# Filler matmuls in and behind the first expert's routing of an attention and mixture-of-experts kernel

## The chip, the cores and the metric

The kernel runs on one core of a Trainium2 chip. The metric is the device time of one execution in microseconds (us). TensorE (PE) does the matrix products, VectorE (DVE) and ScalarE (ACT) the elementwise work, GpSimd (POOL) the indirect transfers, SyncE (SP) issues most of the others. TensorE's clock has two levels, 2.4 GHz (a granted clock of 1.00 in the profile) and 1.2 GHz (0.50).

## The reference

Causal window attention over 8 batches, 8 heads, 576 positions of width 64, followed by a mixture of 8 experts over the 4608 tokens that come out. The experts are filled greedily, best logit first, 576 tokens each:

```python
logits = x @ w_gate                      # x: 4608 x 512, the attention's output
for idx in np.argsort(-logits.flatten()):
    tok, e = idx // E, idx % E
    if assigned[tok] >= 0 or counts[e] >= cap:
        continue
    assigned[tok] = e; counts[e] += 1
for e in range(E):
    mask = assigned == e
    out[mask] = np.maximum(x[mask] @ w1[e], 0.0) @ w2[e]
```

All is in float32. The products of the experts are split in a high and a low part, with three matmuls in place of one.

## The kernel before, in words

The attention runs first, in 36 steps. Then the routing finds which tokens go to which expert, one expert after the other. For expert number p (`Routing.steps`) it searches a threshold in eight rounds (the loop over `r`). In a round of the first expert DVE compares all best logits with 15 candidate thresholds in four pieces (`compare`, line 469), PE counts the hits with 36 matmuls of 8 columns (line 538, into the PSUM tile `rps`), DVE turns the counts into 15x8 flags (`pr`, line 623), one matmul of 8 columns adds them up over the partitions (line 626, tile `h`), and DVE derives the next thresholds from it (lines 641 and 649). Nothing of the next round can begin before that.

After the eight rounds DVE marks the chosen tokens, two matmuls of 72 columns rank them (lines 702 and 703), DVE and ACT spread the ranks into the tiles `A`, `R` and `B`, 18 matmuls of 64 columns make the list (line 744, two halves of nine, each behind its half of `R` and `B`), and eight small ones (line 753) bring it into the form `idx`, by which POOL gathers the expert's 576 rows of x in five transfers (line 1012). PE transposes each gathered tile (line 936), ACT and DVE split it, and the first expert's products follow. From then on the routing of the next experts is recorded between the products of the present one.

While the first expert is routed there is no other work for PE: the attention has ended, and the products wait for the rows. Line 476 (`warm`) fills some of this time. It issues n matmuls of 288 columns whose result nobody reads: 28 behind the list's last matmuls, and 6 behind the transposes of the first gathered tile.

PE runs its instructions in the order in which they are recorded. The order across the concurrent pieces comes from a small planner (`Streams`): each piece is a generator that yields how long it thinks its last work takes. `warm` yields nothing and adds no time to the planner's account. PSUM tiles come from pools with a fixed number of buffers: one `rps` for the routing, three `h` and two `o` for the experts.

Of the kernel before, what the change touches and what calls it, by code (L numbers as in the profile page):

```python
# [9 lines left out]
FT = mybir.dt.float32  # L10
# [15 lines left out]
DM = H * D  # L26
# [265 lines left out]
def consts(tc, cp):  # L292
    nc = tc.nc
    c = dict(pool=cp, zero=cp.tile([128, 128], BF, name="zero"))

    c["jp"] = cp.tile([128, 128], I32, name="jp")
    c["rel"] = cp.tile([128, 128], I32, name="rel")
    nc.gpsimd.iota(c["jp"], pattern=[[1, 128]], base=0, channel_multiplier=-1)
    return c
# [61 lines left out]
class Routing:  # L361
# [107 lines left out]
        self.nc.vector.tensor_tensor(G[:, j0:j1], self.m[:, j0:j1, None].to_broadcast(n),  # L469
                                     thr.bitcast(FT)[:, None, :].to_broadcast(n), OP.is_ge)  # L470

    def warm(self, n):

        x = self.room(128, 288)
        for _ in range(n):
            self.nc.tensor.matmul(x, self.ones, self.r18[:, 0:8], start=True, stop=True)

    def room(self, n, w, spare=False):

        x = self.spare() if spare else self.ps.tile([128, 512], FT, name="rps")  # L480
        return x[0:n, 0:w]
# [12 lines left out]
    def steps(self, p):  # L494
# [8 lines left out]
        if p < E - 1:  # L503
# [19 lines left out]
            for r in range(NR):  # L523
# [71 lines left out]
                if own:  # L595
                    mx = tile_([128, 2], FT, name="mx")
                    nc.vector.tensor_reduce(mx[:, 0:1], cnt, axis=AX.X, op=OP.max)
                    nc.vector.tensor_scalar(mx[:, 1:2], mx[:, 0:1], 0.0, step, op0=OP.is_ge, op1=OP.mult)
                    yield self.dve(350)
                    nc.vector.transpose(pt, mx[:, 1:2].to_broadcast([128, 32]))  # L600
                    d = tile_([128, 1], I32 if r else FT, name="d" if r else "d0")
                    with nc.allow_low_precision(reason="one of 15 multiples of a power of two"):
                        nc.vector.tensor_reduce(d, pt[:, 0:ND], axis=AX.X, op=OP.add)
                    yield self.dve(400) + slack
                    thr2 = tile_([128, ND + 1], I32, name="thr")
                    if r:
                        nc.vector.scalar_tensor_tensor(thr2, self.tab0[:, r + 1], d[:, 0:1],
                                                       base[:, 0:1].to_broadcast([128, ND + 1]),
                                                       op0=OP.bitwise_xor, op1=OP.bitwise_xor)
                    else:  # L610
                        oh = tile_([128, ND], FT, name="oh0")
                        nc.vector.scalar_tensor_tensor(oh, self.dgf, d, thr.bitcast(FT), op0=OP.is_equal, op1=OP.mult,
                                                       accum_out=base.bitcast(FT))
                        nc.vector.tensor_tensor(thr2, self.tab0[:, 1], base[:, 0:1].to_broadcast([128, ND + 1]),
                                                OP.bitwise_xor)
                    base = thr2[:, 0:1]
                    thr = thr2 if r == NR - 2 else thr2[:, 1:]
                    rest = []
                    yield self.dve(300 if r else 500)
                    continue  # L620
                else:
                    pr = tile_([ND, E], BF, name="pr")
                    nc.vector.tensor_scalar(pr, cnt[0:ND], 0.0 if p else float(CAP), step, op0=OP.is_ge, op1=OP.mult)
                    yield self.dve(220) + slack
                    num = self.room(128, E, not p)
                    nc.tensor.matmul(num, self.ones[0:ND], pr, start=True, stop=True)
                    yield self.busy(110) + 200 + slack
                thr2 = tile_([128, ND + 1], I32, name="thr")[:, 0:ND]
                if r == 0:
# [71 lines left out]
        pos = self.room(128, 2 * NJ, not p)  # L701
        nc.tensor.matmul(pos, self.tri, Xf, start=True, stop=False)
        nc.tensor.matmul(pos, self.ones, run, start=False, stop=True)
        yield self.busy(150) + 200 + slack
        Y = tile_([128, 2, NJ], FT, name="Y", bufs=1)
        nc.vector.scalar_tensor_tensor(Y.rearrange("p k j -> p (k j)"), pos, 1.0, Xf,
# [30 lines left out]
        for j0, j1 in ((0, NJ),) if p else ((0, 18), (18, 36)):  # L737
            n = j1 - j0
# [13 lines left out]
            for h in range(2):  # L752
                nc.tensor.matmul(ip[32 * g:32 * g + 32], ils[:, :, h], self.s5[:, h, g], start=(h == 0), stop=(h == 1))
        if p == 0:
            self.warm(28)
        yield self.busy(100) + 200 + slack
        idx = self.rt.tile([128, 5], U32, name=f"idx{p}")
        nc.vector.tensor_copy(idx, ip)
# [58 lines left out]
class Experts:  # L817
# [20 lines left out]

    def room(self):
        return self.ps.tile([128, 320], FT, name="h", bufs=3)  # L840

    def prime(self):

        x = self.fw.tile([8, DM], FT, name="ot", bufs=3)
        self.nc.gpsimd.indirect_dma_start(out=x, out_offset=None, in_=self.xs,
                                          in_offset=IndirectOffsetOnAxis(ap=self.rows[0:8, 0:1], axis=0))
# [460 lines left out]
def body(tc, q, k, v, vt, wg, w1, w2, xs, out):  # L1307
    nc = tc.nc
    with ExitStack() as ctx:
        cp = ctx.enter_context(tc.tile_pool(name="cp", bufs=1))  # L1310
        ctx.enter_context(tc.manual_schedule())
        c = dict(identr=cp.tile([128, 128], FR, name="identr"))
        L = cp.tile([128, NJ, E], FT, name="L")
        rt = Routing(ctx, tc, c, L)
        with ExitStack() as actx:
            ap = actx.enter_context(tc.tile_pool(name="ap", bufs=1))
            c.update(consts(tc, ap))
            wgs = ap.tile([128, HP, 32], FT, name="wgs")
            attention(actx, tc, c, q, k, v, vt, (wgs, wg), xs, L, lambda j0, j1: rt.choices(j0, j1, 0), rt.setup,
                      rt.counters)  # L1320
        rt.start()
        ex = Experts(ctx, tc, c, xs, w1, w2, out)
        rt.spare = ex.room

        st = Streams()
        ex.spawn, ex.busy, rt.busy = st.add, st.busy, st.busy
        ex.clock = rt.clock = lambda: st.now
        ex.warm, ex.rows, rt.prime = rt.warm, rt.rows, ex.prime

        def route():  # L1330
            for p in range(E):
                for dt in rt.steps(p):
                    if p in rt.eint and p not in known:
                        known.add(p)
                        st.add(ex.load(p, rt.eint[p]))
                    if p in rt.idx and p not in listed:
                        listed.add(p)
                        st.add(ex.turn(p, rt.idx[p]))
                    yield dt

        def products():
            for p in range(E):
                yield lambda: p in ex.XT
                yield from ex.steps(p, rt.idx[p])

        known, listed = set(), set()
        st.add(route())
        st.add(products())
        st.run()
# [17 lines left out]
```

## Time and profile before

| what | value |
|---|---|
| median of three runs | 645.01 us (643.61 to 645.83) |
| profiled execution | 644.78 us |
| its span, first to last instruction | 643.1 us |
| mean granted TensorE clock | 0.977 |
| PE busy | 607.8 us, 95% of the span |
| DVE, ACT, POOL busy | 461.0, 340.6, 218.8 us |

The profiled execution takes 1.7 us more than its span. The busy time of PE is an average over three parts: the attention (to about 145 us), the first expert's routing (to about 176 us), and the products of the experts.

### The profile page before, as it was taken

Reading aid. Unit: us, or ns where it says so; the run is one execution under the profiler, and the core shown is the slowest. Engines: PE = TensorE matmul, PEld = TensorE weight load, DVE = VectorE, ACT = ScalarE, POOL = GpSimd, SP = SyncE. Lnnn points to the kernel's source line nnn. Section 1 sums busy time; section 2 is a strip of 40 time slices with the busy share of each in tenths; the row PEclk is TensorE's granted clock in tenths of the full one; section 3 lists DMA queues with packets and bytes.
Section 4 is the critical chain, followed back from the end, with each engine's and each line's share of the span. In section 5 each row is a group of like instructions: output and inputs, shape, how many; then the busy total and the mean of one; then the engine's idle time right before and its main releaser. Section 6 shows DMA issues by size and latency. Waiting matters only on the chain. (4 is left out here: it accounts for less than half of the span.)

```text
span 643.1 us, 16975 instructions
## 1 busy us (share of the span) xinstructions
PE 607.8 (95%) x6423; PEld 524.8 (82%) x6423; DVE 461.0 (72%) x2036; ACT 340.6 (53%) x596; POOL 218.8 (34%) x231
## 2 busy tenths in 40 slices
PE   7899999995599999999999999999999899999995
PEld 6787888774489779978987998798789778888984
DVE  6887888787887768866877786787777844975610
ACT  2576776670255177265555537167345545676720
POOL 4455555550241163042315206124222415023211
PEclk9999999996699999999999999999999989999999
DMA  8997968991476197589669669678929718566811
GB/s 322 380 383 265 364 239 329 372 361 39 161 217 125 53 310 195 115 279 229 146 226 212 172 171 253 168 164 283 210 81 246 181 50 235 168 163 149 167 54 41
DMA packets 39762, 133.06 MB, mean 207 GB/s; under 512 B 5113, under 2 KB 5241, under 8 KB 39681
## 3 DMA queue, kind: packets, MB, share of 16 engines
q0 software_dynamic: 14992, 51.93, 35.1%
q1 hardware_dynamic: 24400, 79.52, 34.2%
q8 instruction: 51, 0.84, 0.5%
q10 hardware_dynamic: 288, 0.52, 0.3%
q14 instruction: 31, 0.25, 0.1%
HBM read 82.15 MB, written 18.87 MB: 157 GB/s over the span
## 5 line engine op out<-in xcount | busy, mean ns | idle before, releaser
L1215 POOL DMA_INDIRECT out<-ot,idx x40 | 41.4, 1035 | 198.7 <-ACT ot L1200 64.0
L1233 PE MATMUL o<-wl,hh 128*128 128x512 f32 x256 | 102.4, 400 | 0.0
L1233 PE MATMUL o<-wh,hh 128*128 128x512 f32 x256 | 102.2, 399 | 0.0
L1233 PE MATMUL o<-wh,hl 128*128 128x512 f32 x256 | 101.8, 398 | 0.0
L144 POOL TENSOR_TENSOR st<-st,mx 128x512 f32<-128x512 f32 x72 | 73.4, 1040 | 65.8 <-DVE mx L137 61.8
L899 ACT ACTIVATE wh<-st 128x1024 fp32r<-128x1024 f32 x72 | 75.6, 1051 | 11.8 <-DMA st<-w 4.5
L910 POOL DMA_DIRECT2D wl<-st x59 | 54.5, 1088 | 73.2 <-ACT wl L908 42.3
L1154 ACT ACTIVATE hh<-h 128x256 fp32r<-128x256 f32 (+1 forms) x96 | 38.9, 407 | 66.4 <-PE h L1186 63.2
L1186 PE MATMUL h<-xh,wh 128*128 128x320 f32 (+1 forms) x384 | 69.9, 301 | 0.7 <-ACT xh L1002 0.7
L1186 PE MATMUL h<-xh,wl 128*128 128x320 f32 (+1 forms) x384 | 70.5, 299 | 0.0
L1186 PE MATMUL h<-xl,wh 128*128 128x320 f32 (+1 forms) x384 | 69.7, 299 | 0.6 <-DVE xl L1006 0.6
L137 DVE CUSTOM_DVE_ANT_0 st<-Sp,mask 128x128 f32<-128x128 f32 x288 | 67.1, 284 | 4.0 <-PE Sp L128 3.2
L1012 POOL DMA_INDIRECT xg<-xs,idx x40 | 43.5, 1086 | 72.0 <-DVE eq L765 61.7
L908 ACT ACTIVATE wl<-wh 128x1024 fp32r<-128x1024 f32 x59 | 62.3, 1056 | 0.8
L1200 ACT ACTIVATE ot<-o 128x512 f32<-128x512 f32 x34 | 20.3, 596 | 76.9 <-PE o L1233 62.8
L1186 PEld LDWEIGHTS h<-xh,wh 128*128 128x128 f32 x384 | 56.8, 189 | 1.4 <-ACT xh L1002 0.8
L1186 PEld LDWEIGHTS h<-xl,wh 128*128 128x128 f32 x384 | 56.9, 189 | 0.9 <-DVE xl L1006 0.8
L1186 PEld LDWEIGHTS h<-xh,wl 128*128 128x128 f32 x384 | 56.9, 189 | 0.2
L1233 PEld LDWEIGHTS o<-wh,hh 128*128 128x128 f32 x256 | 48.4, 189 | 9.9 <-DVE t L1089 0.6
L1233 PEld LDWEIGHTS o<-wh,hl 128*128 128x128 f32 x256 | 48.4, 189 | 9.2
L1233 PEld LDWEIGHTS o<-wl,hh 128*128 128x128 f32 x256 | 48.3, 189 | 9.0
L152 ACT ACTIVATE pt<-Tp 128x512 f32<-128x512 f32 x72 | 39.6, 594 | 19.7 <-PE Tp L150 18.4
(233 smaller groups left out, 1255.9 us busy)
## 6 DMA issues: line engine op xcount, KB each, us to landing
st<-w SPq DMA_DIRECT2D x60, 512.0 KB, 5.8
wl<-st POOLq DMA_DIRECT2D x59, 512.0 KB
V<-v SPq DMA_DIRECT2D x16, 584.0 KB, 7.7
xs<-x SPq DMA_DIRECT2D x36, 256.0 KB, 4.5
VT<-vt SPq DMA_DIRECT2D x8, 640.0 KB, 11.2
VT<-vt SPq DMA_DIRECT2D x8, 512.0 KB, 5.0
Q<-q SPq DMA_DIRECT2D x6, 640.0 KB
K<-k SPq DMA_DIRECT2D x6, 640.0 KB, 8.3
```

Of the source, the lines that this page charges most:

```text
L137: nc.vector.tensor_tensor_reduce(st[:, h, :], Sp[h % 2][:, h // 2], mk, scale=-0.125, scalar=3.0e38, op0=OP.add, op1=OP.min, accum_out=mx[ ...
L144: nc.gpsimd.tensor_tensor(st, st, mx[:, :, None].to_broadcast([128, 4, 128]), OP.subtract)
L152: nc.scalar.activation(pt, Tp, AF.Exp, scale=-1.0)
L899: nc.scalar.activation(hi, x, AF.Copy)
L908: nc.scalar.activation(lo, hi.bitcast(FT), AF.Copy, scale=-1.0)
L910: nc.gpsimd.dma_start(lo.bitcast(FT), x, accum_op=OP.add)
L1012: nc.gpsimd.indirect_dma_start(out=g[0:n, a], out_offset=None, in_=self.xs, in_offset=IndirectOffsetOnAxis(ap=idx[0:n, a:a + 1], axis=0))
L1154: nc.scalar.activation(hh[:, f, c0:c1], h, AF.Relu)
L1186: nc.tensor.matmul(h, wv[:, cc, 128 * (f % 2):128 * (f % 2) + 128], xt[:, cc, c0:c1], start=(k == 0), stop=(k == 11))
L1200: nc.scalar.activation(ot, o, AF.Copy)
L1215: nc.gpsimd.indirect_dma_start(out=self.out, out_offset=IndirectOffsetOnAxis(ap=idx[0:m, a:a + 1], axis=0), in_=ot[0:m], in_offset=None)
L1233: nc.tensor.matmul(o, ht[:, f, 128 * a:128 * a + 128], wt[:, 512 * (f % 2):512 * (f % 2) + 512], start=(f == 0 and k == 0), stop=(f == NF ...
```

## The change

A new function `idle` calls `warm` with an own PSUM tile, one of the two `o`. For the first expert alone it is called in three places: one filler between the count and the sum of a round, six between the sum and the next round's count (three in the first round), and eighteen between the ranking matmuls and the list. The fillers behind the list become 32 in place of 28. Each is a matmul of 128x128 with 288 columns, with a load of its weights. In all 7 x 7 + 4 + 18 + 4 = 75 matmuls and as many weight loads are new.

```diff
-    def warm(self, n):
-        x = self.room(128, 288)
+    def warm(self, n, x=None):
+        x = self.room(128, 288) if x is None else x
         for _ in range(n):
             self.nc.tensor.matmul(x, self.ones, self.r18[:, 0:8], start=True, stop=True)
+
+    def idle(self, n):
+        self.warm(n, self.wide()[:, 0:288])
...
+                    if not p:
+                        self.idle(1)
                     pr = tile_([ND, E], BF, name="pr")
...
                     nc.tensor.matmul(num, self.ones[0:ND], pr, start=True, stop=True)
+                    if not p:
+                        self.idle(6 if r else 3)
...
         nc.tensor.matmul(pos, self.ones, run, start=False, stop=True)
+        if not p:
+            self.idle(18)
...
         if p == 0:
-            self.warm(28)
+            self.warm(32)
...
+    def wide(self):
+        return self.ps.tile([128, DM], FT, name="o", bufs=2)
...
-        rt.spare = ex.room
+        rt.spare, rt.wide = ex.room, ex.wide
```

The instructions of DVE, ACT, POOL and SP stand in the same order as before; on PE the new ones are put in, and nothing else moves. On PE at the end of the first expert's second round (`G` is the tile of comparisons, `one` the choices, `pr` the flags), before:

```order
L538 LDWEIGHTS G
L538 MATMUL rps<-one,G 15x8
L626 LDWEIGHTS ones
L626 MATMUL h<-pr,ones 128x8 [waits DVE_49]
L538 LDWEIGHTS G [waits DVE_49]
L538 MATMUL rps<-one,G 15x8
```

The same place on PE after the change, where lines 542 and 632 are what 538 and 626 were, and line 476 is the filler:

```order
L542 LDWEIGHTS G
L542 MATMUL rps<-one,G 15x8
L476 LDWEIGHTS ones
L476 MATMUL o<-r_466,ones 128x288 [waits PE_49]
L632 LDWEIGHTS ones
L632 MATMUL h<-pr,ones 128x8 [waits DVE_49]
L476 LDWEIGHTS ones
L476 MATMUL o<-r_466,ones 128x288 [waits PE_49]
L476 LDWEIGHTS ones
L476 MATMUL o<-r_466,ones 128x288
...
L542 LDWEIGHTS G [waits DVE_49]
L542 MATMUL rps<-one,G 15x8
```

One filler now stands ahead of the sum and six stand ahead of the next count; the sum and the count still wait for DVE alone.

On PE between the ranking (lines 702 and 703) and the list (line 744), before:

```order
L702 LDWEIGHTS tri
L702 MATMUL h<-X,tri 128x72 [waits DVE_49]
L703 LDWEIGHTS ones
L703 MATMUL h<-run,ones 128x72 [waits DVE_49]
L744 LDWEIGHTS R [waits DVE_49,Activation_49]
L744 MATMUL rps<-B,R 128x64 [waits DVE_49]
```

And after, in the last of the eighteen pairs and behind them (line 754 is what 744 was):

```order
L476 LDWEIGHTS ones
L476 MATMUL o<-r_466,ones 128x288
L476 LDWEIGHTS ones
L476 MATMUL o<-r_466,ones 128x288
L754 LDWEIGHTS R [waits DVE_49,Activation_49]
L754 MATMUL rps<-B,R 128x64 [waits DVE_49]
```

The list's first matmul now stands behind eighteen fillers, which themselves wait for nothing of DVE or ACT.

## Rows read from the trace of the kernel before

**Rows 1.** The page: PE's busy time, and its granted clock in 40 slices.
```profile
PE 607.8 (95%) x6423; PEld 524.8 (82%) x6423; DVE 461.0 (72%) x2036; ACT 340.6 (53%) x596; POOL 218.8 (34%) x231
...
PEclk9999999996699999999999999999999989999999
```

**Rows 2.** Windows, PE alone: stretch, its length, busy (instructions), clock, DMA share, GB/s.
```profile
145.40:149.30 3.90, 1.35 (x39) 1.00 0.19 72
149.40:169.80 20.40, 8.94 (x261) 0.50 0.09 24
169.80:173.20 3.40, 2.96 (x34) 0.50 0.95 353
173.30:176.00 2.70, 2.65 (x22) 1.00 0.83 331
176.00:182.00 6.00, 4.44 (x34) 1.00 0.56 163
182.00:636.00 454.00, 451.27 (x3160) 1.00 0.68 177
```

**Rows 3.** Timeline of PE: start, us, line, operation, [idle before, releaser].
```profile
148.51 0.17 PE L626 MATMUL h<-pr,ones 15*128 15x8 bf16 x1 [0.42 <-DVE pr L623]
149.76 1.05 PE L538 MATMUL rps<-one,G 128*15 128x8 bf16 x36 [1.08 <-DVE G L469]
151.06 0.16 PE L626 MATMUL h<-pr,ones 15*128 15x8 bf16 x1 [0.24 <-DVE pr L623]
152.16 1.05 PE L538 MATMUL rps<-one,G 128*15 128x8 bf16 x36 [0.94 <-DVE G L469]
153.46 0.16 PE L626 MATMUL h<-pr,ones 15*128 15x8 bf16 x1 [0.24 <-DVE pr L623]
154.49 1.05 PE L538 MATMUL rps<-one,G 128*15 128x8 bf16 x36 [0.87 <-DVE G L469]
...
165.09 0.16 PE L626 MATMUL h<-pr,ones 15*128 15x8 bf16 x1 [0.24 <-DVE pr L623]
...
167.17 0.22 PE L703 MATMUL h<-run,ones 128*128 128x72 bf16 x1
169.92 1.14 PE L744 MATMUL rps<-B,R 128*128 128x64 bf16 x18 [2.53 <-ACT R L733]
...
171.54 4.40 PE L476 MATMUL rps<-r,ones 128*128 128x288 bf16 x28
176.00 0.17 PE L783 MATMUL rps<-c,ones 128*128 128x8 bf16 x1
176.43 0.50 PE L936 MATMUL tp<-identr,xg 128*128 128x128 f32 x4 [0.26 <-DMA xg<-xs,idx]
```

**Rows 4.** Timeline of PE elsewhere: fillers at either clock, a later expert's list.
```profile
171.54 1.83 PE L476 MATMUL rps<-r,ones 128*128 128x288 bf16 x7
...
176.83 0.90 PE L476 MATMUL rps<-r,ones 128*128 128x288 bf16 x6
...
226.46 0.70 PE L744 MATMUL rps<-B,R 128*128 128x64 bf16 x18
```

**Rows 5.** Timeline of DVE: what reads the sums and the list, and the list's last input.
```profile
148.72 0.17 DVE L631 TENSOR_REDUCE d<-h 128x1 f32<-128x8 f32 x1 [0.27 <-PE h L626]
...
151.26 0.17 DVE L641 TENSOR_REDUCE d<-h 128x1 int32<-128x8 f32 x1 [0.25 <-PE h L626]
...
169.91 0.45 DVE L721 TENSOR_TENSOR B<-r,sb 128x576 bf16<-128x576 bf16 x1
171.10 0.22 DVE L748 CAST ils<-rps 72x64 bf16<-72x64 f32 x1 [0.74 <-PE rps L744]
```

**Rows 6.** Windows, PE alone, columns as in rows 2: the later fall of the clock.
```profile
511.30:512.90 1.60, 0.00 (x0) 1.00 0.25 56
512.90:514.50 1.60, 1.55 (x9) 1.00 0.72 187
514.60:517.90 3.30, 3.30 (x25) 0.50 0.22 79
```

## The prediction

> **What bounds the kernel now.** I read the page first. PE is busy for 95% of the span, and its granted clock is full except near the 11th and 12th of 40 slices and once later [rows 1]. The windows by stage then tell where PE is not the bound. From 182 to 636 us it is busy 451.27 of 454.00 us [rows 2], so the products can't be shortened by anything done before them: they can only begin earlier or later, and the end moves with them. From 149.4 to 169.8 us PE is busy 8.94 of 20.40 us, at clock 0.50 [rows 2]. That is the first expert's routing, the only thing that runs there.
>
> The timeline of PE shows why it is slow: a round is a ring of waits. The count waits for DVE's comparisons, the sum for DVE's flags (0.24 us), the next count again for DVE (0.87 to 1.08 us) [rows 3]. A round takes 154.49 - 152.16 = 2.33 us, of which PE's records cover 1.21. Behind the ranking PE waits 2.53 us for `R` [rows 3]. The first gathered rows are waited for until 176.43 us, 0.26 us after the last work ahead of them [rows 3]. So the path to the first product is DVE, PE's short matmuls, and then the gather. A microsecond gained or lost there is one at the end.
>
> **The clock.** It was full to 149.3 us although PE was busy only 1.35 of the last 3.90 us; then it was low through rounds in which 36 short matmuls were most of the work; it rose only behind 3.40 us with 2.96 busy (the list and the first fillers) [rows 2]. The late fall is more telling: PE was idle 1.60 us, then busy for 1.55 of 1.60, and still the next 3.30 us ran at 0.50 [rows 6].
>
> **The change, part by part.**
>
> *A filler's price.* At full clock six take 0.90 us with a last one that lasts about 0.28, so (0.90 - 0.28) / 5 = 0.123 us from one to the next. At low clock seven take 1.83 with a last of about 0.42, so (1.83 - 0.42) / 6 = 0.236 us [rows 4]. The loads of their weights run beside them.
>
> *The one between count and sum.* The last count ends at 149.76 + 1.05 = 150.81 and the sum starts at 151.06 [rows 3]. The count's last matmul begins about 0.17 before its end, so the room is 0.42 us; a filler of 0.123 or 0.236 fits at either clock. Even if it had to wait for the last count to end, 0.24 would just fit 0.25. Cost 0, up to 0.1 in the first round, where the tile may still be freed by DVE.
>
> *The six between sum and count.* The room is from the sum to the next count: 154.49 - 153.46 = 1.03 us (1.10 in the round before, 1.25 for the three of the first) [rows 3]. The sum holds the array as long as a count does, (1.05 - 0.17) / 35 = 0.025 us. At full clock 0.025 + 6 x 0.123 = 0.76: hidden by DVE's chain, with 0.27 to spare. At low clock 0.025 + 6 x 0.236 = 1.44: the count comes 0.41 us late, and since its 36 matmuls run without a pause already, the whole lateness stays on the path. There are six such gaps (the six of the eighth round have the 1.7 us to the ranking as cover). Bounds: 0 and 6 x 0.41 = 2.5 us.
>
> *The eighteen.* From 167.17 to 169.92 the room is 2.75 us [rows 3], less some 0.05 for the ranking matmul: 2.70. At full clock 18 x 0.123 = 2.21: hidden. At low clock 18 x 0.236 = 4.25: the list 1.55 us late. Bounds 0 and 1.55.
>
> *What a full clock gives back.* A sum's way to DVE is 148.72 - 148.51 = 0.21 us at full clock and 151.26 - 151.06 = 0.20 at low [rows 3, 5]; the rounds gain nothing by the clock. The list does: 18 matmuls take 1.14 us at low and 0.70 at full clock [rows 3, 4]. Its second half waits for DVE's `B` until 169.91 + 0.45 = 170.36 [rows 5], so only that half counts: now it ends at 169.92 + 1.14 = 171.06, 0.70 after `B`; at full clock a matmul comes every (0.70 - 0.19) / 17 = 0.030 us, nine need 9 x 0.030 + 0.17 = 0.44. Gain 0.26 us. Bounds: 0 (list still at low clock) and 0.3.
>
> The Trainium skill (TensorE: Matmul & The Clock Gate, Single matmul latency) gives a lone matmul a latency of (219 + N) / 1.2 ns at the low and (398 + N) / 2.4 ns at the full clock, an estimate of 189 and 169 ns for 8 columns. By that the count's end and the sum would win 0.02 us each, 0.3 us more over eight rounds. The two rows above don't show it, and the measurement decides: nothing is added.
>
> *The 32 behind the list.* Before, 28 took 4.40 us because the first ones ran at low clock, and ended at 175.94. At full clock 32 x 0.123 + 0.16 = 4.1 us from about 171.3: done at 175.4, ahead of the rows at 176.4. If the clock is low at their start as before, the four more cost 4 x 0.123 = 0.49 and use up the 0.26 us of idle time: 0.2 us late. The small matmul of line 783 behind them is early enough either way.
>
> **The sum.** The profiled execution took 644.78 us, 0.23 under the median of 645.01. Where the attention ends and the first round begins, only four fillers are new, 0.5 us of work in four, so I expect the clock to fall near 149 to 151 us as before. What matters is how long it stays low. A round at low clock then has hardly a pause on PE (the counts' 1.05, fillers of 7 x 0.236 = 1.65, in 2.33 + 0.41 us), like the 3.40 us behind which it rose at 173.2 [rows 2]. So I take one low stretch as long as the late one, 3.30 us [rows 6], or 1.2 to 1.4 rounds. It holds one or two of the six gaps, late by 0.41 each (0.4 to 0.8), and full clock after that gains 0.26: +0.15 to +0.55, mean 0.35. That is 645.1 from the profiled execution and 645.4 from the median; I say **645.2 us**, own range 644.4 to 646.2 with the spread of the runs before (+0.8, -1.4).
>
> **The rivals.**
>
> *The clock goes up and down (slower side).* At full clock a round's records cover 1.05 + 0.12 + 0.16 + 0.74 = 2.07 of 2.33 us, but the counts have 8 columns each and did nothing for the clock in 20 us [rows 2]; the fillers alone are 0.86 of 2.33 us. The late fall came although half of the time before it was dense work [rows 6]. So the clock may fall again as soon as it has risen. With half of the six gaps at low clock: 3 x 0.41 = 1.2; the eighteen with half at low: 9 x 0.236 + 9 x 0.123 = 3.2 against 2.70, 0.5; the gain half lost, -0.1. Together +1.6: 646.4, from 645.4 to 647.3. It decides from the point where the fillers, done in half the time at full clock, no longer hold it. The Trainium skill speaks for it: the same page (A second HAM failure mode: psum-queue depth-cycling) tells of a kernel whose PE paused for moments between groups of matmuls, went to and fro between the levels and lost throughput each time. Rows 6 bear that out in kind; no row shows it for fillers.
>
> *The clock stays low through all rounds (slower).* Six gaps 2.5 and the eighteen 1.55, nothing gained: +4.0, 648.8. For it: the counts never lifted it. Against: fillers at low clock are dense, and such work did lift it at 173.2.
>
> *The clock never falls.* The four fillers of the first round would have to hold it. Then nothing is late and the list gains 0.26: 644.5. Against it: before, it fell behind 1.35 busy of 3.90 us, and the new ones add only 4 x 0.123 = 0.5.
>
> *The gain is larger.* If the gather and all behind it came early by more than the list, say the 0.3 of the latency rule too, it is 644.2. A gain of over 1.94 us has no row to come from, since DVE's own chain fills the rounds.
>
> **How the numbers follow.** One low stretch 0.42, up and down 0.27, never falls 0.18, stays low 0.08, larger gain 0.05. 0.3% of 645.01 is 1.94 us, about what a measurement of this kernel can tell from no change: faster means under 643.07, slower over 646.95. Slower takes all of "stays low" and a quarter of "up and down": 0.15. Faster has only the noise and what I have missed: 0.04. Same 0.81. The range: 643.8 leaves the noise of the fast cases below it, 647.3 leaves "stays low" above.
>
> **What would show it.** In the timeline of PE: rounds of 2.33 us where the clock is 1.00 and 2.7 where it is 0.50; the list starting 2.75 us behind the ranking (right) or 3.2 to 4.3 (wrong); 18 list matmuls in less than 1.14 us; 32 fillers ended before the first gathered rows. In the windows: one low stretch, as long as that of rows 6, between 149 and 156. I am wrong if the rounds are late at full clock, if they get shorter than 2.3 us, or if the start of the products and the end move by different amounts.

## The result and the profile after

The changed kernel takes 650.75 us (four runs, 648.97 to 653.1) against 644.31 of the kernel before in four runs. The ratio is 1.0096, 95% interval 1.0071 to 1.0121, so 4.6 to 7.8 us are lost. In a later set of five runs it was 1.0091 (1.0061 to 1.0122). The profiled execution took 648.97 us. Forecast were 645.2 us and no difference. One run of all those below, of 653.14 us with 2 + 7 fillers, lies over 1.5% above the fastest of its program and is left out of the ratio there.

The page: PE is busy for longer (before: 607.8 us [rows 1]), at the same mean clock, 0.978 against 0.977.

```profile
PE 621.3 (96%) x6498; PEld 531.7 (82%) x6498; DVE 460.6 (71%) x2036; ACT 340.7 (53%) x596; POOL 218.1 (34%) x231
...
PEclk9999999996599999999999999999999999999999
```

The windows of PE tell the stages (columns as in rows 2):

```profile
148.00:150.70 2.70, 1.19 (x42) 1.00 0.28 103
150.80:174.30 23.50, 22.74 (x316) 0.50 0.04 14
174.30:178.00 3.70, 3.70 (x17) 0.50 0.57 151
178.10:184.00 5.90, 5.36 (x62) 1.00 0.83 303
...
190.00:640.00 450.00, 447.75 (x3159) 1.00 0.68 179
```

From 150.8 us, in the first round, through all the others the clock is 0.50, as it was before [rows 2], but PE is no longer idle there: its records cover 22.74 of 23.50 us. It rises at 178.1, behind 3.70 us of the eighteen alone. The products run as before, nearly without a pause.

The timeline of PE, whose rows answer to rows 3 (line 542 counts, 632 sums, 711 ranks, 754 makes the list, 476 is the filler):

```profile
151.17 0.42 PE L476 MATMUL o<-r,ones 128*128 128x288 bf16 x1 [0.36 <-DVE pr L629]
151.52 0.18 PE L632 MATMUL h<-pr,ones 15*128 15x8 bf16 x1
151.64 0.90 PE L476 MATMUL o<-r,ones 128*128 128x288 bf16 x3
152.79 1.05 PE L542 MATMUL rps<-one,G 128*15 128x8 bf16 x36 [0.25 <-DVE G L469]
153.77 0.42 PE L476 MATMUL o<-r,ones 128*128 128x288 bf16 x1
154.13 0.18 PE L632 MATMUL h<-pr,ones 15*128 15x8 bf16 x1
154.25 1.62 PE L476 MATMUL o<-r,ones 128*128 128x288 bf16 x6
155.79 1.05 PE L542 MATMUL rps<-one,G 128*15 128x8 bf16 x36
...
170.83 1.05 PE L542 MATMUL rps<-one,G 128*15 128x8 bf16 x36
...
174.27 0.22 PE L711 MATMUL h<-run,ones 128*128 128x72 bf16 x1
174.31 4.21 PE L476 MATMUL o<-r,ones 128*128 128x288 bf16 x18
178.35 0.69 PE L754 MATMUL rps<-B,R 128*128 128x64 bf16 x18
179.35 0.23 PE L763 MATMUL h<-s,ils 72*32 72x5 bf16 x8 [0.31 <-DVE ils L758]
179.51 4.09 PE L476 MATMUL rps<-r,ones 128*128 128x288 bf16 x32
...
184.08 0.51 PE L949 MATMUL tp<-identr,xg 128*128 128x128 f32 x4 [0.26 <-DMA xg<-xs,idx]
```

Look at what stands in brackets. From the second round's sum on, no count and no sum has a wait for DVE behind it any more: PE itself has become what the round waits for. A round takes 155.79 - 152.79 = 3.00 us. It is made of 0.98 from the first count to the filler, 0.36 to the sum, 0.12 to the six, and 1.54 to the next count, which is 6 x 0.236 and 0.12.

From the attention's last matmul (line 173) to the first of the list's last step (line 753, now 763) the way is 31.41 us. In the profile before it was 26.15, and in a second profile of the same kernel 26.14. The difference of 5.26 us is made of these pieces:

| piece | us |
|---|---|
| six rounds, 170.83 - 152.79 = 18.04 against 14.03 | +4.01 |
| ranking to list, 178.35 - 174.27 = 4.08 against 2.75 | +1.33 |
| the first round, from its first count to the next round's | +0.31 |
| the list to its last step, 1.00 against 1.46 | -0.46 |
| what is left | +0.07 |

Behind the list it is the fillers of PE and the gather that decide, and there two executions of one program differ. The second profile of the kernel before, windows and timeline of PE:

```profile
171.40:177.20 5.80, 5.49 (x44) 0.50 0.95 354
...
172.78 0.23 PE L753 MATMUL h<-s,ils 72*32 72x5 bf16 x8 [0.31 <-DVE ils L748]
172.94 5.69 PE L476 MATMUL rps<-r,ones 128*128 128x288 bf16 x28
...
179.11 0.51 PE L936 MATMUL tp<-identr,xg 128*128 128x128 f32 x4 [0.26 <-issue]
```

Here the clock rose only at 177.2 us, the 28 fillers took 5.69 us instead of 4.40 [rows 3], and no wait for the gathered rows stands before the transposes any more. They start 6.33 us behind the list's last step, against 5.05 in the first profile. In the changed kernel, where the clock is full from the list on, it is 184.08 - 179.35 = 4.73, and 5.45 in a second profile. So a part of what is lost ahead of the list comes back behind it. From the attention's last matmul to the first product it is 38.89 and 38.46 us in the two profiles of the changed kernel, 33.68 and 34.71 in those of the kernel before: 4.5 us by the means.

Between the first profiles the products start 7.92 us later, 2.71 of it because the attention ended later, and the end comes only 4.2 us later (spans of 647.3 and 643.1). The prediction had named such a difference as a sign of being wrong. It lies in the first profile of the kernel before: from the first product to the end that one has 464.19 us, its second profile 461.05, and the changed kernel 460.47 and 461.09. Of the excess 1.6 us is the late fall of the clock [rows 6] and 1.5 stands between the transposes at 519.84 and 564.63 us; neither is in the second profile, nor in those after.

### The profile page after: what moved, and what is told of

It is laid out like the page before. It is cut to its first block, busy times and chain, and to the rows that moved or that the text cites. A ratio compares the mean times of both kernels' runs of the same rounds, so it can differ in the third digit from the quotient of the medians.

```text
span 647.3 us, 17124 instructions
## 1 busy us (share of the span) xinstructions
PE 621.3 (96%) x6498; PEld 531.7 (82%) x6498; DVE 460.6 (71%) x2036; ACT 340.7 (53%) x596; POOL 218.1 (34%) x231
```

## The experiments

Theory A: the clock stays at 1.2 GHz in the rounds, the fillers there are longer than the gaps, and PE bounds the rounds. Theory B: a filler costs by its number, its weight load and its waits, at any clock. Theory C: the loss is outside the routing. All ratios are against the kernel before on the same chip, with 95% intervals; "the way" is the one of 26.15 us from above, to the list's last step, in the experiment's profile.

**One part alone: the rounds' fillers.**

```diff
-            self.idle(18)
...
-            self.warm(32)
+            self.warm(28)
```

> Only the fillers between the rounds (1 + 6, and 1 + 3 in the first); none ahead of the list, 28 behind it as before. Theory A (the fillers run at the low clock and are longer than the gaps): clock 0.50 through all rounds, a round 3.01 us as in the changed kernel instead of 2.33, the list starts 3.1 us behind the ranking as before; the time is 4 to 4.5 us over the kernel before, ratio 1.006 to 1.007. Theory C (the loss is not in the routing: the attention ends 2.7 us later because of the new PSUM use): the first count starts at about 148.1 again instead of 145.4 and the time is 6 us or more over the kernel before.

Ratio 1.0062 (1.0039 to 1.0086). Rounds of 3.01 us at clock 0.50, the list 2.75 us behind the ranking, the way 30.39 us (+4.24). Its 28 fillers behind the list ran at the low clock for 5.70 us, as in the second profile of the kernel before. A is met.

**One part alone: the eighteen.** The calls between the rounds are taken out, and 28 stand behind the list.

> Only the eighteen fillers between ranking and list; none between the rounds, 28 behind the list. Theory A: clock 0.50 through the rounds, rounds 2.33 us; the list starts 4.3 to 4.5 us behind the ranking instead of 2.75, its 18 matmuls then take 0.7 instead of 1.14 us; 1.3 lost, 0.4 won back: about 0.9 us over the kernel before, ratio 1.001 to 1.002. Theory C: the first count at about 148 and 2.5 us or more over the kernel before.

Ratio 0.9995 (0.9972 to 1.0019): no difference that can be told. The profile shows the expected pieces, in the timeline of PE:

```profile
170.08 0.22 PE L707 MATMUL h<-run,ones 128*128 128x72 bf16 x1
170.12 4.27 PE L476 MATMUL o<-r,ones 128*128 128x288 bf16 x18
174.22 0.69 PE L750 MATMUL rps<-B,R 128*128 128x64 bf16 x18
```

The list starts 4.14 us behind the ranking, a little less than expected, and is made in 0.69 instead of 1.14 us; the way is 27.08 us (+0.93). Most of this comes back behind the list, where the clock is full already: from the attention's last matmul to the first product it is 34.55 us, between the two values of the kernel before.

**One part alone: 32 behind the list.** All calls of `idle` are taken out.

> Only the 32 fillers behind the list in place of 28; no others. The prediction's price: four more, 0.5 us, of which 0.2 is late: ratio 0.999 to 1.002. If more than 1 us is lost, the part of the change's loss that the runs with the rounds' fillers alone and the eighteen alone leave over stands here.

Ratio 1.0009 (0.9982 to 1.0036), the way 26.13 us. The four more are not where the loss is. The three parts alone add up to 0.7% with wide intervals, the change costs 0.9 to 1.0%; the runs can't tell whether the 0.2 to 0.3% between them stands in their meeting.

**The attention's end.** The kernel before once more.

> The kernel before once more, for a second profile. If the 2.7 us by which the attention ended later in the changed kernel's profile is a matter of the execution and not of the change, the first count here starts later than 145.4 us too, at 147 to 148.5, and the way from it to the list's end stays at 26.0 us (the ranking 2.75 us ahead of the list). If it is the change's (theory C), the first count starts within 0.5 us of 145.4.

The first count is at 146.79 us, between what was expected of the two theories; with the rounds' fillers alone and the eighteen alone it had been at 147.67 and 148.30, near C's 148.1. The attention's last matmul starts at 146.64 us, against 145.23 in the first profile of the same program. In the changed kernel it is at 147.94 and 146.95, and in the six experiments above and below without a bridge at 147.11 to 148.28. The one with 32 behind the list, which has no new filler until long after, is at 147.46. So most of the 2.7 us is the execution's; a smaller shift by the change isn't excluded by two profiles of the kernel before. The way to the list is 26.14 us. Theory C falls as the main cause, since the rounds' fillers alone cost 0.62% and the pieces of the way account for most of the rest.

**Less: fillers that fit at the low clock.**

```diff
-                    if not p:
-                        self.idle(1)
...
-                        self.idle(6 if r else 3)
+                        self.idle(3)
...
-            self.idle(18)
+            self.idle(9)
...
-            self.warm(32)
+            self.warm(28)
```

> Fillers cut to what fits at the low clock with 0.1 us for each change between a short matmul and a filler: none between count and sum, 3 between sum and count (0.95 of 1.03 us), 9 ahead of the list (2.4 of 2.75 us), 28 behind it. Theory A (only fillers longer than the gap at the low clock cost): clock 0.50 through the rounds, rounds of 2.33 us, the list 2.75 us behind the ranking; no difference from the kernel before, ratio 0.999 to 1.001. Theory B (each filler group costs, wherever it stands): rounds of 2.5 us or more, 1.5 us or more over the kernel before.

Ratio 1.0014 (0.9990 to 1.0037). The timeline of PE at clock 0.50 (line 630 sums):

```profile
156.51 0.16 PE L630 MATMUL h<-pr,ones 15*128 15x8 bf16 x1 [0.24 <-DVE pr L627]
156.60 0.90 PE L476 MATMUL o<-r,ones 128*128 128x288 bf16 x3
157.53 1.05 PE L542 MATMUL rps<-one,G 128*15 128x8 bf16 x36
158.83 0.16 PE L630 MATMUL h<-pr,ones 15*128 15x8 bf16 x1 [0.24 <-DVE pr L627]
```

The wait for DVE ahead of the sum is back, a round takes 2.32 us, the way 26.07. The 24 fillers of the eight rounds cost nothing here, and gain nothing. In this profile PE waited 1.24 us for the first gathered rows, and the clock fell once more at 180.6, among their transposes.

**The same number, half as long.**

```diff
-            self.nc.tensor.matmul(x, self.ones, self.r18[:, 0:8], start=True, stop=True)
+            self.nc.tensor.matmul(x, self.ones, self.r18[:, 0:x.shape[1] // NJ], start=True, stop=True)
...
-        self.warm(n, self.wide()[:, 0:288])
+        self.warm(n, self.wide()[:, 0:144])
```

> The whole change with fillers of 144 columns in place of 288 between the rounds and ahead of the list: the same number of matmuls and weight loads, in the same places (32 of 288 behind the list). Theory A (length at the low clock): the clock is 0.50 through the rounds, six half fillers and two changes are 0.12 + 5 x 0.12 + 0.25 = 0.97 of 1.03 us, so rounds of 2.33 to 2.4 us and the list 2.75 us behind the ranking: ratio 0.999 to 1.002. Theory B (each filler costs by its number, its weight load and wait): rounds of 2.7 us or more and 3 us or more over the kernel before.

Ratio 1.0013 (0.9993 to 1.0033). Every matmul, weight load and wait of the change is there, at clock 0.50, and the loss of 0.9% on the same chip is gone. A window and the timeline of PE:

```profile
151.10:169.10 18.00, 16.20 (x310) 0.50 0.05 19
...
155.38 0.16 PE L632 MATMUL h<-pr,ones 15*128 15x8 bf16 x1
155.48 0.90 PE L476 MATMUL o<-r,ones 128*128 128x144 bf16 x6
156.41 1.05 PE L542 MATMUL rps<-one,G 128*15 128x8 bf16 x36
157.40 0.30 PE L476 MATMUL o<-r,ones 128*128 128x144 bf16 x1
157.71 0.16 PE L632 MATMUL h<-pr,ones 15*128 15x8 bf16 x1
```

Rounds of 157.71 - 155.38 = 2.33 us, the way 26.17. Theory B falls: it is the length, not the number. (The 32 behind the list, still of 288 columns, took 6.43 us at the low clock in this profile.)

**The changed kernel again**, as the measure for the last one.

> The changed kernel again, on the chip of the two next ones. Theory A: low clock (28 us and more of it) in nearly all executions, rounds of 3.01 us, ratio 1.007 to 1.010. If some executions hold the clock, they are 5 us or so faster than the others.

1.0091, as said; a round takes 3.01 us, the way 30.78. None of its five runs held the clock: by the mean clock of each (span x (1 - clock) x 2) they had 27 to 34 us at the low one.

**More: twelve in place of six.**

```diff
-                        self.idle(6 if r else 3)
+                        self.idle(12 if r else 3)
```

> The changed kernel with 12 fillers in place of 6 between sum and count. Theory A: where the clock is 0.50 a round takes 3.01 + 6 x 0.236 = 4.4 us; if the denser work lifts the clock, a round at 1.00 takes about 0.89 + 0.41 + 0.12 + 12 x 0.123 + 0.09 = 3.0 us. All rounds at the low clock: 8.5 us over the changed kernel, some 660; lifted after two rounds: about that of the changed kernel, 650 to 654. If the rounds take 3.0 us at clock 0.50, their length is not the fillers' and theory A is wrong.

Ratio 1.0091 (1.0052 to 1.0130): twice the fillers cost no more than the change. The windows and the timeline of PE show why:

```profile
153.00:156.20 3.20, 3.20 (x39) 0.50 0.02 5
156.40:175.00 18.60, 18.35 (x307) 1.00 0.01 2
```

```profile
153.97 0.18 PE L632 MATMUL h<-pr,ones 15*128 15x8 bf16 x1
154.08 2.71 PE L476 MATMUL o<-r,ones 128*128 128x288 bf16 x12
...
158.02 0.16 PE L632 MATMUL h<-pr,ones 15*128 15x8 bf16 x1
158.11 1.64 PE L476 MATMUL o<-r,ones 128*128 128x288 bf16 x12
...
160.98 0.16 PE L632 MATMUL h<-pr,ones 15*128 15x8 bf16 x1
```

The clock rises at 156.3, among the first twelve fillers, and stays up. A round takes 4.05 us at the low and 160.98 - 158.02 = 2.96 at the full clock, as A said (4.4 and 3.0; the rise falls into the long one). The way is 30.95 us: one round of 4.05 and five of 2.96 against six of 3.01, while the eighteen, now at the full clock, hide ahead of the list.

**Holding the clock.** A bridge of 26 matmuls of 128 columns stands between the attention's last matmul and the first round's counts, which have time there, and eight fillers behind the first round's sum. Three versions: 1 + 6 fillers a round, 2 + 7 (its edit is shown), and 3 + 8.

```diff
+    for _ in range(26):
+        nc.tensor.matmul(SB[1][:, 0, 0:128], z, z, start=True, stop=True)
     for m, x in stores:
         store(m, x)
...
-                        self.idle(1)
+                        self.idle(2 if r else 1)
...
-                        self.idle(6 if r else 3)
+                        self.idle(7 if r else 8)
```

> The changed kernel with a bridge into the rounds: 26 fillers of 128 columns right behind the attention's last matmul (1.5 us of work, ahead of the first round's 32 counts, which wait for nothing of it), and 8 in place of 3 in the first round; 1 + 6 in the others, 18, 32. Theory A: the clock is still 1.00 when the second round starts, and a round at 1.00 takes 2.33 to 2.4 us (fillers hidden); where it falls in spite of the 7 fillers a round, the rounds after it take 3.01. Theory B (a filler costs its weight load and its change of operands at any clock): rounds of 2.7 us or more also at 1.00.

> The bridge (26 matmuls of 128 columns behind the attention) with 2 + 7 fillers a round: at the full clock with 0.1 us for each change, 0.43 of 0.42 us and 1.07 of 1.03 us. Theory A: clock 1.00 through all rounds in most executions (mean clock 0.99 and more), rounds of 2.35 to 2.45 us, ranking to list 2.75 to 3.0; against the kernel before 7 x 0.07 = 0.5 us lost in the rounds and 0.4 won at the list: ratio 0.999 to 1.002. If it is slower by 2 us or more with the clock held and rounds under 2.45 us, something else than the rounds costs there.

> As the run with the bridge, but 3 + 8 fillers a round in place of 1 + 6 (at the full clock 0.37 of 0.42 us and 1.0 of 1.03 us of the gaps). Theory A: the clock stays 1.00 from the attention to the products, rounds 2.33 to 2.5 us, the list's 18 matmuls 0.7 us, the 18 ahead of it hidden; the time is between 0.3 us under and 1.5 us over the kernel before. If the clock falls all the same, rounds of 4 us and 8 us or more over the kernel before. Theory B: rounds of 3 us at 1.00.

Ratios 1.0037 (1.0011 to 1.0064), 1.0026 (0.9993 to 1.0060) and 1.0052 (1.0033 to 1.0072). What they teach is in the executions of one and the same program, which differ by whether the clock held:

| fillers a round | mean clock | times, us |
|---|---|---|
| 1 + 6 | 0.998, 0.992 | 642.24, 643.67 |
| 1 + 6 | 0.984 to 0.985 | 645.93, 646.42, 646.91, 648.36 |
| 1 + 6 | 0.977 to 0.980 | 647.04, 648.28, 648.95, 649.38 |
| 2 + 7 | 0.994 to 0.997 | 642.94, 643.21, 643.42, 645.06, 645.61, 646.00 |
| 2 + 7 | 0.977 | 650.18 |

The same instructions cost 5.5 us more (1 + 6, by the means of the first and the third row) and 5.8 (2 + 7, a single run) where the clock is low. By the mean clock alone that is no proof of the place, but it is about the size of the loss on the way. The ratio of 2 + 7 is above the 1.002 expected; the six runs that held the clock have a median of 644.2 us, against 644.39 of the kernel before. One more run of 2 + 7 had a mean clock of 0.907 and 650.68 us; where it lost its clock isn't known. In the profile of 1 + 6 the clock held through the rounds, fell ahead of the list and again among the first products (windows of PE, columns as before):

```profile
149.00:166.80 17.80, 17.20 (x336) 1.00 0.06 19
167.00:170.30 3.30, 3.00 (x15) 0.50 0.09 12
...
180.60:183.90 3.30, 3.27 (x17) 0.50 0.72 181
```

The first window holds the changed kernel's rounds, 1 + 6 fillers and 37 short matmuls each: where the clock was full, it stayed so for 17.8 us. Its timeline has the round that the change would have at the full clock:

```profile
152.69 0.16 PE L634 MATMUL h<-pr,ones 15*128 15x8 bf16 x1
152.78 0.91 PE L478 MATMUL o<-r,ones 128*128 128x288 bf16 x6
153.72 1.05 PE L544 MATMUL rps<-one,G 128*15 128x8 bf16 x36
154.70 0.30 PE L478 MATMUL o<-r,ones 128*128 128x288 bf16 x1
155.01 0.16 PE L634 MATMUL h<-pr,ones 15*128 15x8 bf16 x1
```

155.01 - 152.69 = 2.32 us, the way 26.03: hidden, as the prediction had it, and nothing gained over 26.15 but 0.12. With 2 + 7 a round takes 2.40 us and the way 26.55. With 3 + 8 the clock was high in all nine runs (0.989 to 0.999), and a round takes 2.65 us, the way 28.09; there A's numbers were missed (up to 2.5 us a round and 1.5 us over the kernel before; the medians are 3.2 apart), since three and eight fillers with their changes no longer fit even at the full clock. Its timeline of PE:

```profile
155.58 0.17 PE L634 MATMUL h<-pr,ones 15*128 15x8 bf16 x1
155.68 1.15 PE L478 MATMUL o<-r,ones 128*128 128x288 bf16 x8
156.77 1.05 PE L544 MATMUL rps<-one,G 128*15 128x8 bf16 x36
157.75 0.54 PE L478 MATMUL o<-r,ones 128*128 128x288 bf16 x3
158.22 0.17 PE L634 MATMUL h<-pr,ones 15*128 15x8 bf16 x1
```

From sum to count it has 0.10 + 1.09 us instead of 1.03, with no wait for DVE. This profile also waited 2.36 us for the first gathered rows, which its fillers don't explain and which the runs leave open. No version beats the kernel before by what can be measured.

## Why the prediction was wrong

**The step that failed** is "I take one low stretch as long as the late one": the choice between its cases. The way from rounds to products, the gaps, and the price of a filler were read from the right rows; the case "the clock stays low through all rounds" is what happened: 0.50 for 27.3 us, from 150.8 to 178.1, in place of 3.30. It had been put at 648.8 and given 0.08.

1. *That the clock falls near 149 to 151*: right, 150.8.
2. *That fillers at the low clock lift it again*: wrong. The argument was that PE then has hardly a pause, like the stretch before the rise at 173.2 [rows 2]. The records cover 22.74 of 23.50 us and the clock stayed at 0.50. What had stood before that rise were matmuls of 64 and 288 columns (and eight of 5); 37 of the 44 matmuls of a round have 8 columns, and their records, 0.17 us long and 0.025 apart, overlap and so cover the time. The prediction had said itself that the counts "did nothing for the clock in 20 us", but only against the case at the full clock. In all three profiles of 1 + 6 fillers a round without a bridge the clock stayed at 0.50 through these rounds; it rose while fillers alone ran in a row: the eighteen ahead of the list (at 178.1 and 175.9 us in the two profiles of the change), the 28 behind it (182.4, the rounds' fillers alone), or the twelve (156.3). With the bridge the same round, begun at the full clock, kept it in the profile. Which property of the mix made the difference no run took apart. The 3.40 us too were one execution's: in the second profile of the kernel before the clock rose behind 5.80 us, 5.49 of them busy.
3. *The price of a late round*: 0.41 expected, 0.67 measured (3.00 against 2.33). The sum had no term for the changes. Between sum and count 1.44 was worked out and 0.12 + 1.54 = 1.66 measured: 0.12 us where a filler follows the short matmul, and about as much where a short one follows the filler. These 0.22, and 0.04 more around the one filler, are the rest. The run with half fillers shows 0.10 at the change into its six, hidden in the gap; what follows them is covered by the time of DVE.
4. *The eighteen*: room 2.70 and 4.25 at the low clock, +1.55; measured +1.33, since the clock rose for the last of them, and +0.84 in the second profile, where it rose earlier.
5. *The gain of the list*: 0.26 expected, 0.46 measured. With the list late, neither of its halves waited for `B`, and all 18 ran at the full clock. Where the list was on time at the full clock (2 + 7 and 3 + 8 fillers), it was 0.23 and 0.24, close to that.
6. *The first round*: 0 to 0.1 expected, 0.31 measured. By its row the filler between count and sum was let go by DVE only with `pr`, and so stood right in front of the sum, 0.35 us.
7. *That the rounds gain nothing by the clock*: right, 2.32 us at full against 2.33 at low. The Trainium skill's latencies (TensorE: Matmul & The Clock Gate, Single matmul latency) would have, as an estimate, the count's end and the sum 0.02 us faster each; no more than 0.01 in a round is seen. So the 0.3 us by that estimate, which the rival of a larger gain was given, is in no run.
8. *Up and down*: not seen in the changed kernel. It came with the bridge, where 1 + 6 fillers held the clock in two of ten runs, by the mean clock.
9. *The 32 behind the list*: 4.1 us at the full clock expected, 4.09 measured. That the gathered rows, and not the fillers, end the wait there was read from one execution; in the second profile of the kernel before it is not so.

With the case right and the sizes as they were, the forecast would have been 648.8, just under the lowest of the four runs; with 0.26 more in each of six rounds it is 650.4, near their median. That closeness is partly luck: points 4 to 6 (-0.22, -0.46 and +0.31 us on the way) are left out of it, and so is what comes back behind the list.

## What to carry to other kernels

Work put in to keep the clock up must fit its gap at the low clock, with some 0.1 us for each change between short and long matmuls as measured here; sized for the full clock it becomes the bound just where it is needed. Before adding it, look whether a full clock would pay there: here a round is bound by DVE, and holding the clock gave back a tenth of a microsecond on the way to the list. Where a case of low chance has the largest price and one mechanism decides it, ask which rows speak of that mechanism alone; here none did: the rise at 173.2 had no counts just ahead of it, the rounds before had no fillers, and both were read from one execution.

## What the runs showed of the hardware

- PE's records covered 97% of 23.5 us (22.74) at a granted clock of 0.50 all through, with 37 matmuls of 8 columns and 7 of 288 in a round; in another run the same rounds kept a clock of 1.00 for 17.8 us. A timeline without gaps did not tell the clock here.
- A change between a matmul of 8 columns and one of 288 costs about 0.1 us at either clock: 0.12 us each at the low one, and in the run with 3 + 8 fillers at the full one 0.10 into the group and 1.09 - 8 x 0.123 = 0.11 out of it. The weight loads there are recorded with 0.10 and 0.11 us, which would fit; no run took that apart.
- Executions of one program differ: the kernel before had runs from 640.81 to 649.83 us over the sets on three chips, at mean clocks of 0.97 to 0.98. A stage that ends 2 us early or late in one profile is no cause yet.
